# Another order of 1287 jobs in a sketched attention with attention experts behind it

## The chip, the core and the metric

The kernel runs on one core of a Trainium2 chip. Five engines work in parallel, each through its own list of instructions: PE (the tensor engine, with a separate row PEld for its weight loads), DVE (the vector engine), ACT (the scalar engine), POOL (GpSimd) and SP (which here only issues DMA transfers; ACT issues a few too). Engines wait for one another by semaphores. The metric is the device time of one execution in microseconds, lower being better.

## The reference

Two stages in float32. The first is an attention without softmax over sketched features, for 4 batches, 4 heads, 1088 positions and 32 dimensions; the second, on its output, is a layer of 4 attention experts of which every position uses two.

```python
def phi(x):                                   # r = 8, so 64 features
    a = np.einsum('rd,bhsd->bhsr', S1, x)
    b = np.einsum('rd,bhsd->bhsr', S2, x)
    return np.einsum('bhsi,bhsj->bhsij', a, b).reshape(*x.shape[:-1], r * r)
q_p, k_p = phi(q), phi(k)
kv = np.einsum('bhsf,bhsd->bhfd', k_p, v)
z = np.sum(k_p, axis=2)
x = num / (den + 1e-6)                        # num = q_p @ kv, den = q_p @ z
x = x.transpose(0, 2, 1, 3).reshape(4, 1088, 128)

logits = x @ w_gate                           # 4 experts, the best two
w = exp(sel - max(sel)); w /= w.sum(-1) + 1e-9
for e in range(4):
    q, k, v = x @ wq[e], x @ wk[e], x @ wv[e]
    a = causal softmax of q @ k.T / 8
    out += w[e, where chosen] * (a @ v @ wo[e])
```

The output is 4 x 1088 x 128.

## The kernel before

**A plan of jobs.** The kernel's body emits nothing at first. It describes 1287 jobs in a `Plan` (from line 64): each has a name, the engine or the two engines it may run on, the values it reads and makes, and the buffers it holds. Then `plan.run(ORDER)` (line 1316) walks a hand-placed string (lines 21 to 56) and emits the jobs in that order. A word of it is a job's number; a letter b behind it picks the second of the job's engines. An engine's program is thus the part of the list that falls to it, in the list's order, and the engine keeps to that order: an instruction that waits holds up all that stands behind it on the same engine. Buffers come from small pools (4 pairs of PSUM banks "ps", 6 row buffers "w", 3 "in", 3 "qs", 3 "mb", 2 "xT", 2 "AT", 2 "agg", 2 "ob" and so on). A job that first uses a buffer takes the one longest free, so the list also decides which buffer each job gets and whose release it waits for. The compiler adds separate event-semaphore instructions where an instruction has to wait for more than it can carry itself.

**The stages of a batch.** The jobs' names are used below.

- *Sketched attention.* "load k", "load q", "load v" (lines 429, 437, 457) bring rows in; "turn k" and "turn q" (490, 494) transpose them on DVE; "sketch" (524, PE) applies S1 and S2; "back" (527, DVE) transposes the sketches; in batches 1 to 3 "add low" (548, POOL) adds the two halves of the keys' sketch; "features" (532, POOL or DVE) forms the 64 products; "sums" (576, PE) gives kv and z; "numer" (635 or 771, PE) and a division give x. x is kept transposed ("xT") and is also stored to a scratch in memory and fetched back in another layout ("xra", "xrb", "xrc").
- *Gate.* "logits" (822 and 829, PE), "turn logits" (833, DVE), "choose" (856 to 872, DVE) finds the two experts, "maximum", "exponents" and "shares" (875 to 902) the weights, "turn choice" (922 to 926), and the choice goes through memory to become masks "mb" (947, 950). "gate order" (294, 295, POOL) brings the columns of `w_gate` ("wgr") into the order the gate uses.
- *Experts.* Rows go in tiles of 64, 17 a batch, in three groups: tiles 0 to 5, 6 to 11, 12 to 16; the last batch takes them in the order second, third, first. For each group "query" (1018, PE) multiplies x by a product of wq and wk for all four experts, "base" (a copy) and "pick" (1031, DVE) select by the masks. Then for each tile: "score" (1056, PE), "take" (1068, DVE: mask and running maximum), "exp" (1084, ACT), "guard" (1090 on ACT or 1092 on POOL: adds 1e-9), "invert" (1095, DVE), "weigh" (1099, POOL: times the inverse and the gate's share), "turn A" (1104, DVE: a 32 x 32 block transpose into "AT"). The group's "sum" jobs (1132, PE) multiply AT with x; they need all tiles of their group. "keep V", "patch V", "spread V", "mix V" (1162 to 1175) sort the results by expert, "out" (1210, 1236, 1260, PE) multiplies by a product of wv and wo, and the result is copied and stored.

Batches overlap: the sketched attention and the gate of a batch are woven into the experts of the batch before.

**The head of the list.** Among the first jobs are the loads, eight "dummy" jobs (251, two matmuls on zeros each), and setting-up work on POOL: constants, "pick8" (340 to 345), the mask (287, 290), "rep16" (348) and "skx" (349), clearings (479), and the gate order, which waits for the transfer of `w_gate` (271). In the compiled program a transfer waits for the one issued eight earlier.

**The names by number.** In a name such as "take 2.15.0" the first number is the batch, the second the tile and the third the part of the row; in "pick 0.1.1" and "sum 2.1.0" the second is the group.

Of the kernel before, what the change touches and what calls it, by code (L numbers as in the profile page):

```python
# [18 lines left out]


ORDER = """
1 3 0 2 48 76 77 4 74 51 37b 75 10a 60 46 52 84 50 81 54 49 88 8a 45 89 7a 17a 85 22a 78 80 97 86 79 53 87 400 98 100a
397 90 55 99 91 92 63b 83a 64 391 102a 47 101b 96a 392 66 103b 24a 19a 59 82a 65 67a 401 114 115a 396 39b 108 95a 94a
110 111a 93a 403 56 109a 112 113a 105 104 106a 394 116 58 402 406 107b 57 122 408 407 123 395 410a 117a 68 126 118 69
413a 409a 127 119 399a 61 128 120 398a 393 70 414b 124 129a 412a 405 416 121b 125a 411a 62a 415 404 146 147 152 688 148
154 417a 693 162 418 163 153 149 179 180 183a 155 150 424 425a 156 158 151 167 184a 131 168 181 157a 170 130 689 169
159a 185 419 182 426 186 201 700 164 9b 174 215 175 427 133 202 208 132 165 428 203 209 176 216 204a 171 429 205 430 246
222 245 166a 435 210 211a 223 436 217 187 206 694 172 431 207 433a 177 212 250a 691 194 432a 18a 249a 195 137 318 160
173 218a 188 319 247 699 697 437 189 219 213 196 248 161a 251 690 438a 197a 434 252 439a 323a 322a 190a 703 421 422 191
224 192 692 220 268 214 704 420 705 193 423 706a 267 71 698 134 72 269 276 707a 275 440 710a 73 277 135 270 324 320 225b  # L30
221 198 321 271b 708a 199 226 292 227 272 291 325 23b 278 695a 696a 293 200 178a 273 441 145 442a 31b 253 136 702 228
274 283 711a 443a 254 701 294 279a 28b 284 709a 260 326 280 327 295a 261 285 461 296 462 262 712 255 328 329 713 281
714a 229 230 330b 231 715 256a 297 263b 721 463 286 282 464 233b 466 235a 257 264 359 258 465 358 722a 471 716 298 140
234a 351 265 360 232a 141 237 236 259 238 266 350 989 334 335 467 287a 139 352 720 985 472 361 138 342 343 239 362 16b
331 723 468 288 336 344 353 289 363 332 991 290 476 479 337 724 345 477 725 333 364a 354b 355 480a 481b 726 478 356 365
299 14b 300 301 302 303 304 338a 482 483 143 241 346a 306a 366 339 340 732 990 444 142 367 448 307a 305a 718 341 473 347
447 445 733 505 446 474 308b 240 242 348 309 311 310 727 512 986 728 506 519 243b 994 312 513 545 520 514 349 498 499
515a 988 357 544 521 144 314 729a 491 516 996 313 38b 315 469 507 543 15b 542 734 992b 316a 546a 997 492 508b 475a 493
735a 494a 20b 517 368 26b 522a 736a 369 509 370 495 500 993a 371 372 451 719 547b 501b 29b 548 523 717 373 524 510 374
375 518 450 449 737 376 730b 484 731 549 525 377a 496 379a 502 503 244 378b 497 380a 485 383 589 588 486 550 382 381 738  # L40
452 511 11b 590 551 572 573 740a 564 574 384 487a 504 739a 565 488 575 576a 580 581 566 1000 489 582 758 615 490 591 577
1002 1004b 616 470 583 618 759 552 459 617 567 1001 526 568a 619a 578 1008a 592a 620a 584b 527 987 25b 762 1007b 1003a
569 453 621 768 579 1006a 528 529a 585 557 622 553a 530a 32b 531a 1005b 558 760 623 33b 593 624 317 625 586 533 761 385
1010 534 570 559 386 763 594 1009 626 1011a 627a 536 769 764 532b 554 535 587 648 1012 647 571 560a 639 628 640 649 595
765 774 999 629 631 561 630 562 458 641 632 460 773 778a 656 642 655 455 555 776 775 633 538 657 770 777a 643a 1013 563
634 995 650 658 644 779 651a 780 539 659 556 537 771 635b 540a 795 802 796 645 456 636 41b 387 652 653 660 454 1014 661a
803 637 646 662 816 1018 596 663 654 597 817 1019b 598 599 998 664 781 457 638 788 782 789 818 600 601 741 790 665 772a
804 819a 12b 602b 797 745 603b 744 791b 604a 820 541 792 605a 666 805b 607 821 742 608 806 667 606 1020 609 390 822 807
668 783 1017 1021 1022 40b 743 669 388 1023 670 766 1024 27b 1029 751 839 809 810 840 784b 1025 671 672 1030 43b 673 747
785 1026a 844a 808 748 841 843a 1027a 1031 1028 793 675a 786 842 1016 811 787 798b 676a 845 812a 612 677a 1015 1033a  # L50
1032a 749 846 389 13b 674a 794 756 813 678 679 611 799 800 854 885 1034 855 610 613a 750 35b 886 887 861 862 888 847 863
848 814 681 864 1035 1037b 815 878 801 680 856 877 870 869 849 34b 754 889b 857a 746 879 850a 913 912 871 1036a 1055 823
824 916b 872 1056 865b 1057 1058 890 851 1059 825 873a 6b 1065 917b 866 767 880 914 829a 1066 757 827a 915 918 752 858
828a 867 826a 881b 868 859 682 852 891 919 882 929 1060 830 853 928 937 874 892 875 831 936 883 1061 945 683 833 930 884
931 938 832 920 876 932b 921 753 953 614 922 860 21b 944 946 952 939 1063 947 1142 923 954 1141 1067 955 933 948a 1146a
1143 956 1144 893 949 1145a 686 1038 934 957 958a 894 940a 1039 1147 1148 959 960 895 935 896 897 898 901a 1172 1171 755
924b 950 900a 925 961 1041 42b 941 951 904 834 899a 835 926 1164 1163 902a 44b 927 1173 905 903 1040 1187 1042 1165 1149
1150 1188 1156 1189 36b 942 836 1190 906 1174 1191b 1215 943 1068 684 837b 1069a 687 1180 1151 1157 1158 1179 1192 1217
1181 1214 1159b 1216 962 1064 1182 963 1219b 1183b 964 1152b 965 1166 1044 1175a 1193 838 966 1160 1153 1167b 967 1184
1218a 1161 1220 1194 968 1185 969 1221 970 1168 1176 1222 1162 685 972a 973a 976 1255 971b 974a 1045 1154 1254 977 975  # L60
978 1177 1223 1155 1256 1257 1258 1230 1224 1178 1259 1047 1247 1225 1231 1246 1169 1071 1052 1046 1070 1248 1062 1186
907 1260a 1073 5b 1051 1232 1226b 1075a 1072 1043 1261 1262 909 1048 1074b 1238 1227 1249 908 1170 1076 1228 1050 1233
1077 1239 1106 1234a 910a 1240 1235 1229 1085 979 1236 1086 1107 911 1241 1250a 980 1242b 1251 1243 1108 1244 1245 1263
1113 1099 1195 1109a 1049 1252 1196 1100 1114 30b 1197 1087 1088a 1253 1198 1237 1078 1092 1054 1093 1115 1094 1079 1199
1200 1201b 1095b 1264 1096 1080 1265 1205 1266 1267 1204b 1116b 1110 1081b 1268 1053 1089 1117 1269 1082 983 1083 1202b
1090 1101 1203b 1111 1207 1091 1084 1270 1206 1208 981 1102a 1271 1103 1272 1118 1209 1112 1119 1210 1097 1273a 1274a
1104 1098 1105 982 1211 1278 1275b 1120 984 1121 1276a 1122 1123a 1277 1128 1279 1125 1280 1281 1126a 1212a 1127a 1213
1124 1131 1132 1133 1129 1282 1284 1283 1130a 1134 1139a 1285 1135b 1286 1140b 1136a 1137b 1138a
""".split()


# [1278 lines left out]
```

## Time and profile before

| what | value |
|---|---|
| runs | 259.37, 260.77 and 422.44 us, median 260.77 |
| the profiled execution's own time | 260.19 us |
| its span, first to last instruction | 258.5 us |
| granted clock of the tensor engine | 1.00 |
| PE idle, from the span | 9.1 us |
| the four largest lines on PE | L1056 73.7 us, L1132 44.6 and 27.2, L1018 34.3 |
| moved by transfers | 27.88 MB in 40381 packets |

The profile is of one execution. Its page gives busy time for each engine, the span in slices, the chain of work that ended last and the costliest groups of instructions; the trace behind it answers questions on stretches of time, on one line of the code or on one engine. "L1056" is a line of the kernel as it was before; in the changed kernel every line behind the list is one larger, since the list has one line more. Matmuls overlap one another, so a busy PE is not a PE at its peak.

### The profile page before, as it was taken

The numbers are of one execution on the slowest core, as the hardware profiler recorded it, in microseconds if no ns is written. First come the engines' busy times: TensorE is split into PE (matmuls) and PEld (weight loads), VectorE is DVE, ScalarE is ACT, GpSimd is POOL, SyncE is SP. The second block draws the span as 40 slices with busy tenths as digits, with TensorE's granted clock in tenths as the row PEclk, the third lists the DMA queues.
The fourth block names the chain that finished last, engine by engine and source line by source line (L and its number), as shares of the span: only waits on it lengthen the run. The fifth ranks groups of instructions, "written<-read, shape, count | busy, mean of one in ns | idle before, by whom it ended". The sixth has DMA issues, their size and how long they took to land.

```text
span 258.5 us, 9931 instructions
## 1 busy us (share of the span) xinstructions
PE 249.4 (96%) x4159; PEld 185.6 (72%) x4161; DVE 207.2 (80%) x527; ACT 108.0 (42%) x287; POOL 157.8 (61%) x265
## 2 busy tenths in 40 slices
PE   7888998999999999999999999999999999999995
PEld 2467654576598896665799776765896975789994
DVE  6969899998987886999997387999888638878332
ACT  4346445872803505840634044624624316432110
POOL 6718489958489754577663976087366634533742
PEclk9999999999999999999999999999999999999999
DMA  6936379205827552702612694304252157430003
GB/s 212 240 98 174 92 195 252 45 3 127 215 54 147 126 146 79 193 3 82 172 32 38 125 249 126 84 18 140 42 90 76 53 136 184 110 60 3 3 4 86
DMA packets 40381, 27.88 MB, mean 108 GB/s; under 512 B 25872, under 2 KB 35600, under 8 KB 40336
## 3 DMA queue, kind: packets, MB, share of 16 engines
q1 hardware_dynamic: 39888, 26.62, 42.8%
q8 instruction: 32, 0.52, 0.9%
q10 hardware_dynamic: 448, 0.62, 0.7%
q14 instruction: 13, 0.11, 0.1%
HBM read 22.62 MB, written 4.62 MB: 105 GB/s over the span
## 4 chain that ended last, share of the span: by engine, by line
PE 83%; DMA 6%; DVE 5%; POOL 2%; issue 2%; ACTq 0%; ACT 0%; DVEq 0%; POOLq 0%
PE pair L1132 30%; PE pair L1056 26%; PE pair L1018 9%; PE pair L1260 7%; PE pair L1210 3%; DMA wgr<-in_moe_w_gate_dram 2%; DMA w<-in_v_dram 2%; PE pair L771 2%; POOL fp L532 2%; DMA in<-in_q_dram 2%; PE pair L524 1%; PE pair L576 1%; DVE qs L1031 1%; PE pair L1236 1%; PE pair L822 1%
## 5 line engine op out<-in xcount | busy, mean ns | idle before, releaser
L1099 POOL TENSOR_SCALAR w<-w,rs,sh 128x960 f32<-128x960 f32 (+15 forms) x68 | 56.5, 837 | 32.1 <-DVE rs L1095 29.5
L1056 PE MATMUL pair<-xT,qs 128*128 128x320 f32 (+11 forms) x216 | 73.7, 478 | 1.3 <-DVE rs L1095 0.7
L1084 ACT ACTIVATE w<-w,mx 128x768 f32<-128x768 f32 (+16 forms) x68 | 52.3, 769 | 48.0 <-DVE mx L1068 44.3
L1068 DVE CUSTOM_DVE_ANT_0 w<-pair,mask 128x192 f32<-128x192 f32 (+14 forms) x68 | 48.3, 723 | 11.3 <-PE pair L1056 9.1
L1056 PEld LDWEIGHTS pair<-xT,qs 128*128 128x128 f32 x216 | 38.3, 190 | 26.5 <-issue 10.9
L1104 DVE STREAM_TRANSPOSE AT<-w 128x64 f32<-128x64 f32 (+15 forms) x68 | 50.7, 758 | 4.6 <-POOL w L1099 4.5
L1132 PE MATMUL pair<-AT,xra 32*128 32x160 f32 (+5 forms) x1136 | 44.6, 302 | 0.0
L1132 PEld LDWEIGHTS pair<-AT,xra 32*128 32x128 f32 x1136 | 41.8, 185 | 3.7 <-issue 1.5
L1166 POOL TENSOR_TENSOR agg<-agg,mb 128x768 f32<-128x768 f32 (+1 forms) x22 | 33.9, 1557 | 13.0 <-ACT agg L194 8.8
L1018 PE MATMUL pair<-xT,Mq 128*128 128x384 f32 (+1 forms) x96 | 34.3, 477 | 0.1
L194 ACT COPY agg<-pair 128x384 f32<-128x384 f32 (+1 forms) x34 | 14.1, 464 | 48.4 <-PE pair L1132 45.5
L532 POOL TENSOR_TENSOR fp<-w 128x576 f32<-128x576 f32 x22 | 26.6, 1223 | 2.8 <-DVE w L527 1.8
L1132 PE MATMUL pair<-AT,xrb 32*128 32x160 f32 (+5 forms) x752 | 27.2, 288 | 0.0
L1132 PEld LDWEIGHTS pair<-AT,xrb 32*128 32x128 f32 x752 | 26.3, 185 | 0.8 <-issue 0.7
L1031 DVE COPY_PREDICATED qs<-mb,pair 128x768 f32<-128x768 uint16 (+1 forms) x24 | 23.1, 964 | 2.6 <-DMA mb<-me 1.2
L1018 PEld LDWEIGHTS pair<-xT,Mq 128*128 128x128 f32 x96 | 17.3, 190 | 10.0 <-issue 2.1
L1260 PEld LDWEIGHTS pair<-Mo,agg 128*128 128x128 f32 x168 | 20.6, 192 | 3.2 <-issue 1.4
L1260 PE MATMUL pair<-Mo,agg 128*128 128x128 f32 x168 | 21.3, 277 | 0.0
L1092 POOL TENSOR_SCALAR rs<-zs 128x1 f32<-128x1 f32 x28 | 6.3, 226 | 20.8 <-ACT w L1084 17.9
L1162 DVE COPY_PREDICATED agg<-mb,pair 128x384 f32<-128x384 uint16 (+1 forms) x24 | 12.8, 554 | 6.5 <-ACT agg L194 6.3
L194 ACT COPY qs<-pair 128x384 f32<-128x384 f32 (+1 forms) x18 | 7.8, 459 | 16.4 <-PE pair L1018 16.4
L527 DVE STREAM_TRANSPOSE w<-pair 128x576 f32<-128x576 f32 x16 | 11.6, 755 | 3.2 <-PE pair L524 3.0
(173 smaller groups left out, 288.6 us busy)
## 6 DMA issues: line engine op xcount, KB each, us to landing
xra<-xd SPq DMA_DIRECT2D x16, 192.0 KB, 4.6
xrb<-xd SPq DMA_DIRECT2D x16, 192.0 KB, 4.8
xrc<-xd SPq DMA_DIRECT2D x16, 160.0 KB, 4.6
in<-in_k_dram SPq DMA_DIRECT2D x7, 272.0 KB, 4.4
mb<-me SPq DMA_DIRECT2D x3, 576.0 KB, 6.1
mb<-me SPq DMA_DIRECT2D x6, 288.0 KB, 3.9
in<-in_q_dram SPq DMA_DIRECT2D x3, 544.0 KB, 6.4
xd<-w SPq DMA_DIRECT2D x12, 136.0 KB, 3.1
```

The lines of the kernel that those rows point to most:

```text
L194: (nc.scalar.copy if eng == "ACT" else VEC[eng].tensor_copy)(o, i)
L532: VEC[e].tensor_tensor(out=f, in0=a[:, :, None, R : 2 * R].to_broadcast([128, NJ, R, R]), in1=a[:, :, 0:R, None].to_broadcast([128, NJ, R, ...
L1018: nc.tensor.matmul(plan[ps[x]][:, y, 0:w], Mq[:, ((1, 2), (0, 3))[x][y]], plan[xT][:, 64 * t0 : 64 * t1], start=True, stop=True)
L1031: nc.vector.copy_predicated(chosen(), c, rows(plan[ps[x]]))
L1056: nc.tensor.matmul(plan[p][:, y, 0 : c1 - c0], plan[qs][:, 128 * t : 128 * t + 128], plan[xT][:, c0:c1], start=True, stop=True)
L1068: nc.vector.tensor_tensor_reduce(out=o, in0=src, in1=msk, scale=-1.0, scalar=mx[:, b, i, x - 1 : x] if x else 3e38, op0=ALU.add, op1=ALU.m ...
L1084: nc.scalar.activation(out=a, in_=a, func=ACTF.Exp, bias=mx[:, b, i, last : last + 1], scale=-1.0, accum_out=zs[:, b, i : i + 1])
L1099: nc.gpsimd.tensor_scalar(out=a, in0=a, scalar1=rs[:, b, i : i + 1], scalar2=plan[("sh", b)][:, i : i + 1], op0=ALU.mult, op1=ALU.mult)
L1104: nc.vector.transpose(dst[:, 0 : keys // 32, t], plan[A][:, 0:keys].rearrange("p (j s) -> p j s", s=32))
L1132: nc.tensor.matmul(plan[Vk[g // 2]][:, g % 2, lo : 32 * nt], plan[(f"xr{j // 12}", b)][rows, j % 12], a[rows, j, lo:], start=(j == 0), sto ...
L1166: nc.gpsimd.tensor_tensor(out=a, in0=a, in1=masks_in(plan[mb], w)[:, 2 * x : 2 * x + 2], op=ALU.mult)
L1260: nc.tensor.matmul(plan[p][0:m, 0, 128 * x : 128 * x + 128], plan[agg][:, e, 128 * x : 128 * x + m], Mo[:, e], start=(e == 0), stop=(e == ...
```

## The change

Only the string `ORDER` is replaced. It holds the same 1287 jobs in another order, some with another letter: 15 guards move from ACT to POOL and 14 from POOL to ACT, seven "keep V" copies from ACT to DVE and nine back, five "base" copies from ACT to DVE and two back, and a few features, spreads, scalings and stores change sides. One dummy job more runs on PE (dummy18). No other line differs. The first and last lines of the two lists:

```diff
 ORDER = """
-1 3 0 2 48 76 77 4 74 51 37b 75 10a 60 46 52 84 50 81 54 49 88 8a 45 89 7a 17a 85 22a 78 80 97 86 79 53 87 400 98 100a
-397 90 55 99 91 92 63b 83a 64 391 102a 47 101b 96a 392 66 103b 24a 19a 59 82a 65 67a 401 114 115a 396 39b 108 95a 94a
...
-1104 1098 1105 982 1211 1278 1275b 1120 984 1121 1276a 1122 1123a 1277 1128 1279 1125 1280 1281 1126a 1212a 1127a 1213
-1124 1131 1132 1133 1129 1282 1284 1283 1130a 1134 1139a 1285 1135b 1286 1140b 1136a 1137b 1138a
+2 1 3 44b 76 77 0 45 74 401 46 75 48 52 8a 49 17a 78 79 7a 51 54 85 88 84 80 4 81 89 22a 50 86 34b 87 10a 97 98 90 64
+100a 53 99 91 391 19a 92 394 102a 63a 96a 395 402 59 101b 24a 56 82a 392 66 103b 83a 65 67a 95b 94a 93a 114 115a 403 110
...
+1207 981 1274a 1208 1119 1209 1275b 1278 1211 1084 1273a 1210 1120 1277 1121 1276b 1122 984 1212a 1123a 1280 1279 1128
+1125 1124 1281 1127a 1213 6b 1126a 1131 1129 1282 1284 1286 1130a 1132 1133 1134 1139a 1283 1135b 1137b 1285 1140b 1136a
+1138b
 """.split()
```

What the new list moves around the places of which the prediction speaks, by the lists of the engines:

- On SP, the load of `w_gate` (job 56) is the 14th transfer instead of the 16th, the two halves of batch 1's keys (jobs 391 and 392) the 11th and 15th instead of the 13th and 14th. Three more loads go by ACT in both.
- On POOL, the gate order stands ahead of pick8, the mask, rep16, skx and the clearing of batch 1's keys instead of behind them.
- On DVE, "take 2.15.0", "take 2.16.0", "choose b3.0" and "keep V 2.0.1" stand between "pick 2.2.0" and "turn A 2.7".
- At the end, ACT issues two of the last three stores, and SP one, instead of one and two.

More of the change, by code (lines that the diff above doesn't have):

```diff
@@ L27 @@
[L27 to L61, printed above, removed]
@@ L67 @@
-1104 1098 1105 982 1211 1278 1275b 1120 984 1121 1276a 1122 1123a 1277 1128 1279 1125 1280 1281 1126a 1212a 1127a 1213
-1124 1131 1132 1133 1129 1282 1284 1283 1130a 1134 1139a 1285 1135b 1286 1140b 1136a 1137b 1138a
+2 1 3 44b 76 77 0 45 74 401 46 75 48 52 8a 49 17a 78 79 7a 51 54 85 88 84 80 4 81 89 22a 50 86 34b 87 10a 97 98 90 64
+100a 53 99 91 391 19a 92 394 102a 63a 96a 395 402 59 101b 24a 56 82a 392 66 103b 83a 65 67a 95b 94a 93a 114 115a 403 110
+57 108 112 113a 111a 105 397 104 109a 58 396 400 107b 116 60 47 406 106b 55 122 408 407 68 393 123 117a 126 410a 413a
@@ new lines @@
+118 127 398a 119 61 70 399a 414b 69 128 409a 120 412a 405 62a 121b 129a 691 124 416 411a 125a 415 404 146 689 147 154
+152 148 179 162 180 153 155 417a 150 130 149 694 418 163 183a 424 131 156 425a 688 151 167 168 158 164 170 184a 181 169
+692 174 182 157a 159a 426 700 185 18a 175 30b 132 186 427 419 201 215 693 165 428 245 696a 187 202 216 171 423 133 176
+203 429 208 204a 435 166a 172 430 177 188 431 217 205 246 436 209 249a 250a 699 206 697 218a 222 207 33b 210 211a 194
+36b 195 422 248 432a 223 160 433a 247 219 319 437 212 213 161a 695a 196 135 420 438a 189 23a 439a 251 318 434 252 703
@@ new lines @@
+173 690 214 190b 323a 322a 267 704 197a 224 268 705 71 191 706a 198 708a 269 72 192 709a 324 440 270 193 199 271a 276
+275 277 272 178a 200 321 421 137 225b 273 226 73 227 136 278 291 320 707a 292 441 325 293 220 228 443a 284 134 279a 701
+442a 711a 283 698 274 260 280 285 221 991 294 261 710a 327 144 326 286 253 328 262 295b 287b 461 140 712 990 296 288 329
+254 713 281 702 289 255 31b 986 714b 994 229 297 263a 230 715 26b 231 716 462 721 463 256a 282 233a 264 464 235a 722a
+138 298 39b 359 232a 358 141 290 237 466 257 234a 360 989 351 14b 236 350 258 265 259 361 335 334 342 352 343 238 142
@@ new lines @@
+465 139 330b 12b 336 337 362 717 331 344 345 723 266 239 353 724 479 476 332 471 478 43b 725 472 477 299 363 333 726
+481a 364a 444 300 467 27b 985 480a 301 302 346a 468 727 482 338a 339 347 732 473 348 303 733 354a 304 365 483 447 734
+445 307a 13b 340 474 242 349 240 735b 355 306a 305b 356 310 341 308a 309 241 519 446 357 448 512 311 312 491 243a 366
+987 545 544 143 492 505 513 315 988 514 515a 475b 520 145 314 367 313 469 521 506 522a 523 498 316a 719 543 728 730b 317
+542 493 494a 507 499 368 720 547b 508a 369 370 495 736b 737 524 516 729a 40b 996 500 517 718 449 546b 496 371 372 373
@@ new lines @@
+455 374 997 375 376 454 525 501b 497 548 378a 549 518 509 731 484 377a 457 5b 485 993b 379a 510 502 381 451 380a 450 589
+588 382 486 503 504 590 550 487a 488 551 738 511 572 384 573 565 489 740b 574 564 739a 581 566 580 567 575 582 1000 9b
+583 591 383 490 568b 758 1002 615 759 762 1004a 552 576a 768 1001 616 1003b 618 458 592b 452 470 1006b 617 456 526 569
+760 620a 577 459 1007b 619a 578 593 621 527 769 622 992a 579 528 557 531a 532a 1005a 530a 1008a 534 584b 558 529b 594
+533 585 559 385 761 624 595 648 623 570 244 386 647 1010 625 626 553b 1009 560b 763 586 535 627a 649 764 628 587 650 571
@@ new lines @@
+640 639 536 773 561 651a 554 1011b 641 632 775 631 774 629 630 655 1012 656 765 20b 652 555 562 776 642 633 453 460 643a
+556 537 778a 563 657 539 634 644 777a 390 635a 1013 538 779 770 995 780 658 540a 795 1017 636 389 999 659 802 796 645
+803 660 637 653 646 804 816 1018 596 597 1016 1019a 771 661b 797 662 817 638 37b 788 654 789 772b 781 818 819b 598 663
+790 599 600 601 664 782 665 602a 666 604a 667 798b 1015 741 820 821 783 745 603b 799 16b 668 791a 606 605a 607 998 1020
+742 541 822 669 744 609 1021 608 792 1023 1022 743 793 839 766 809 1024 1029 840 805a 843b 747 670 810 1025 1014 784a
@@ new lines @@
+671 672 1027a 1026a 751 673 785 811 806 786 844b 841 1030 1031 842 845 1028 611 794 612 812a 677a 610 1033a 846 862
+1032a 674a 678 755 28b 676b 861 675a 1034 813 613b 807 814 863 800 787 847 679 387 815 864 848 885 886 1035 748 865b 680
+854 887 1036a 808 801 878 877 870 681 746 849 855 888 1037a 869 614 889b 879 912 871 752 880 913 1055 850a 917b 749 890
+1056 856 823 824 872 881a 866 867 1057 873b 1059 882 916b 874 825 767 851 914 918 42b 868 875 876 915 682 919 852 891
+937 936 853 883 1058 1065 756 827a 826a 830 829b 944 683 928 831 929 945 892 857a 750 753 828a 858 833 884 938 952 35b
@@ new lines @@
+930 953 1060 920 939 1061 859 832 946 1066 955 41b 921 954 931 932b 922 860 1144 32b 1141 1143 947 956 948a 940a 923
+1142 949 1067 941 933 893 957 1146a 950 1063 924b 25b 894 895 951 942 1068 388 1145a 925 1038 896 897 934 958b 11b 1147
+959 898 902a 960 1148 835 900a 686 926 1172 1040 901b 943 899a 836 905 903 904 935 1163 1164 1156 1165 906 1039 961 927
+1166 834 754 837a 1171 1173 1042 1187 1179 684 15b 1041 1157 1180 1181 1188 1189 38b 1182 1149 1174 1215 1214 1216 1150
+1167a 757 1217 1190 1064 1219a 962 1069b 963 1158 964 1218b 965 1151 1183a 966 1191a 1184 1168 967 968 1159b 969 1175a
@@ new lines @@
+1220 1169 1185 1176 970 1152b 1160 1221 1177 1186 1178 974a 973b 972a 971a 1223 1044 1254 1222 1161 977 975 1162 1257
+976 978 1047 1192 1224 1255 1225 1256 838 1070 1258 1071 1170 1193 1153 1231 1046 1154 1230 1247 1075b 1246 1074b 1259
+1194 908 1155 907 1248 1260a 909 1261 1226b 1227 685 1053 1073 687 1062 1052 1232 1072 1076 1043 1238 1233 1249 1077
+1239 910b 1050 1240 1228 1049 1262 1234b 1085 1045 1235 1229 1250a 1236 1086 1241 1242b 1106 1107 1251 979 29b 1252 980
+1263 1048 1108 1243 1099 1100 1109b 1087 1244 1253 1113 1195 1196 1197 1245 1198 1110 1078 1237 1114 1101 1115 1102b
@@ L69 @@
+1092 1093 1199 1200 1111 1103 1204a 1051 1079 1088b 1116a 1264 1089 1104 1265 1266 1105 1054 1202b 1201a 1205 1267 1112
+1268 983 1117 1269 1094 1095b 1080 1096 982 1270 1081a 1082 1271 1272 1118 1090 1097 911 1203a 1083 1091 1206 1098 21b
+1207 981 1274a 1208 1119 1209 1275b 1278 1211 1084 1273a 1210 1120 1277 1121 1276b 1122 984 1212a 1123a 1280 1279 1128
+1125 1124 1281 1127a 1213 6b 1126a 1131 1129 1282 1284 1286 1130a 1132 1133 1134 1139a 1283 1135b 1137b 1285 1140b 1136a
+1138b
 """.split()
```

8 lines of the change are left out of this document (removed).

## The prediction

> **What bounds the kernel now.** I read the page's first part and its chain by engine, then the windows of five microseconds, then the chain in order of time.
>
> ```profile
> span 258.5 us, 9931 instructions
> PE 249.4 (96%) x4159; PEld 185.6 (72%) x4161; DVE 207.2 (80%) x527; ACT 108.0 (42%) x287; POOL 157.8 (61%) x265
> PE 83%; DMA 6%; DVE 5%; POOL 2%; issue 2%; ACTq 0%; ACT 0%; DVEq 0%; POOLq 0%
> ```
>
> The tensor engine (PE) is busy for 249.4 of 258.5 us and is 83% of the chain that ended last. An average hides stages, so the windows come next; the columns are PE, weight load, DVE, ACT, POOL, granted clock, DMA share and GB/s.
>
> ```profile
> 30.00:35.00 5.00, 4.44 (x74) 2.30 (x74) 4.80 (x15) 1.50 (x4) 3.25 (x13) 1.00 0.23 55
> 35.00:40.00 5.00, 4.95 (x22) 3.11 (x23) 4.92 (x22) 4.12 (x16) 4.57 (x10) 1.00 1.03 282
> 40.00:45.00 5.00, 4.23 (x50) 2.18 (x49) 4.89 (x9) 2.12 (x9) 5.00 (x9) 1.00 1.13 235
> 45.00:50.00 5.00, 5.00 (x77) 2.81 (x75) 5.00 (x12) 3.73 (x9) 4.67 (x8) 1.00 0.36 64
> 205.00:210.00 5.00, 5.00 (x161) 4.96 (x153) 0.84 (x4) 0.00 (x0) 0.84 (x2) 1.00 0.66 169
> 210.00:215.00 5.00, 5.00 (x17) 2.82 (x16) 3.84 (x9) 1.48 (x4) 3.74 (x4) 1.00 0.24 72
> 250.00:255.00 5.00, 5.00 (x39) 4.33 (x37) 2.66 (x5) 1.34 (x3) 1.83 (x2) 1.00 0.23 56
> ```
>
> All 42 windows from 45 to 255 us, of which four stand here, have PE at 5.00. Ahead of 45 us PE has holes and DVE is full (4.80, 4.92, 4.89). So there are three stages: a head, a long stage in which PE never stops, and a tail. The chain in order of time gives the joints.
>
> ```profile
> 10.79 5.82 DMA wgr<-in_moe_w_gate_dram
> ...
> 19.59 0.80 POOL w L548
> ...
> 25.35 0.83 PE pair L576 x67
> ...
> 26.62 0.39 DVE ch L833
> ...
> 42.45 1.24 PE pair L1056 x4
> ```
>
> The gate's weights land at 10.79 + 5.82 = 16.61. POOL then prepares the keys of batch 1 from 19.59 on (add low, features), the sums at 25.35 need them, the first gate logits follow, and DVE turns these at 26.62. From there DVE works without a pause until the query selection "pick 0.1.1", which the scores at 42.45 wait for. From 42.45 on PE runs through. A reordering can therefore win in the 42 us of the head and in the last 3 us. In between it can only lose, unless PE's own instructions get shorter or fewer.
>
> **The change part by part.** The listings of the two compiled kernels show the same 1287 jobs. PE has one dummy more and otherwise the same jobs: 258 from "sketch k2" on in both, 136 of them at the same place, the others moved by one place in the mean and eight at most, with 48 changes of tile mode in both. About 60 jobs change their engine: 15 guards go from ACT to POOL and 14 back, and DVE gets 391 jobs instead of 384. The event-semaphore instructions are 43 instead of 48 on PE, 101 instead of 98 on DVE, 77 instead of 65 on ACT.
>
> *The head's transfers and POOL.* Among all loads (three go by ACT) the gate's weights are the seventeenth instead of the nineteenth; the halves of batch 1's keys, which were sixteenth and seventeenth, are fourteenth and eighteenth. POOL takes up the weights first, and only then does five jobs that stood ahead of them.
>
> ```profile
> 8.91 0.88 SPq L429 DMA_DIRECT2D in<-in_k_dram  x2
> 10.24 0.33 SPq L437 DMA_DIRECT2D vr<-in_v_dram  x1
> ```
> ```profile
> 16.16 1.37 DVE L490 STREAM_TRANSPOSE in<-in 128x544 f32<-128x544 f32 x2 [1.08 <-DMA in<-in_k_dram]
> ```
> ```profile
> 0.79 0.11 POOL L340 MEMSET pick<- 128x16 f32 x1 [0.29 <-POOLq L1334]
> ...
> 1.67 0.20 POOL L345 MEMSET S2r<- 128x128 f32 x1
> ...
> 5.46 0.95 POOL L287 MEMSET mask<- 128x1024 bf16 x1
> 6.48 0.52 POOL L290 TENSOR_SCALAR_AFFINE_SELECT mask<-mask 64x64 bf16<-64x64 bf16 x2
> ...
> 12.19 0.15 POOL L479 MEMSET in<- 128x64 f32 x1
> 12.28 0.84 POOL L348 COPY rep<-SK 32x256 f32<-32x256 f32 x1
> 13.07 0.73 POOL L349 COPY skx<-SK 128x32 f32<-128x32 f32 x1
> 16.66 0.18 POOL L294 COPY wg<-wgr 128x2 f32<-128x2 f32 x1 [2.87 <-DMA wgr<-in_moe_w_gate_dram]
> 16.78 0.18 POOL L295 COPY wg<-wgr 128x2 f32<-128x2 f32 x1
> ```
>
> The seventeenth issue is the second of the pair at 8.91, so about 8.91 + 0.44 = 9.35. With the same 5.82 of flight the weights land at 15.17. Behind that wait POOL now has: the gate order (16.66 to 16.96, 0.30), the repeated sketch and skx (12.28 to 13.80, 1.52), a clearing (0.09, from 12.19 to the next start), the pick matrix and S2r (0.79 to 1.87, 1.08) and the mask (5.46 to 7.00, 1.54). That is 4.53 us, so add low starts at 15.17 + 4.53 = 19.70 instead of 19.59: +0.1. If the transfer lands where it did, the start is 16.61 + 4.53 = 21.14, +1.6. The keys are the other limit. Their second half went out at 9.35, and DVE turned both halves at 16.16 when they were there, so 6.81 later; now it goes out in the eighteenth slot, 10.24: 17.05, 0.9 later. The turning of the first half no longer stands behind that wait, so only half of 1.37 follows it: ready at 17.05 + 0.69 = 17.74 instead of 17.53, and add low with it at 19.59 + 0.2 = 19.8. If the keys' flight is shorter now that their halves are apart, nothing but the sketch and the weights limits, and I bound that gain at 0.5, a slot between two issues (10.79 − 10.24). I take the later of the two limits, +0.2, because the lists move the starts and the rows give the flights. The five POOL jobs from add low on keep their order.
>
> *DVE from the first gate logits to pick 0.1.1.* It does the same 34 jobs in another order, with nine semaphore instructions ahead of them instead of eight.
>
> ```profile
> L1056 PEldq EVENT_SEMAPHORE  x5: 51/51/51, 96.2 to 223.1; - x5
> ```
> ```profile
> L1068 DVEq EVENT_SEMAPHORE  x44: 21/21/1605, 38.0 to 234.1; - x44
> ```
>
> These are the least, median and longest nanoseconds; the 1605 is a wait, the 21 the instruction. One more is +0.02. In the three windows from 30 to 45 DVE idles 0.20 + 0.08 + 0.11 = 0.39, so no order of the same jobs can win over 0.4 there; a new wait in it could cost, which is a rival. I take 0.0.
>
> *PE from 42.45 on.* The same work, back to back. From "sketch k2" on two semaphore instructions fewer, at the 51 ns of such a row: −0.1. If PE's queue takes them during running matmuls it is nothing; if all five saved counted it would be −0.26. The Trainium skill ("Perfetto Trace Analysis", Identifying Dependency Chains) says that instructions that wait on several engines may get event-semaphore instructions inserted ahead of them. By that rule the twelve more on ACT and three more on DVE are real waits of several engines and not only 21 ns each; the trace's row agrees in so far as 21 is the usual price and 1605 has been seen.
>
> *The extra dummy* lies ahead of the scores at 42.45, where PE idles 0.56 + 0.05 + 0.77 = 1.38 us between 30 and 45.
>
> ```profile
> L251 PE MATMUL pair<-idle 128*128 128x512 bf16 x14 | 5.1, 499 | 1.5 <-DVE idle L244 1.2 <-DVE w L527 0.3
> L1092 POOL TENSOR_SCALAR rs<-zs 128x1 f32<-128x1 f32 x28 | 6.3, 226 | 20.8 <-ACT w L1084 17.9 <-ACT rs L1090 1.5
> ```
>
> Its two matmuls cost 2 x 0.50 = 1.0 us and fit in: nothing. If the holes are gone, +1.0. *The engine swaps*: one guard more on POOL at 0.23 us, seven jobs more on DVE at its mean of 207.2 / 384 = 0.54, 3.8 us on an engine that idles 258.5 − 207.2 = 51 us. PE's stream covers them; where that cover is thin is the second rival.
>
> *The tail.* Before, SP issues the first two of the last three stores and ACT the third; now ACT issues two.
>
> ```profile
> 255.50 0.83 SPq L1242 DMA_DIRECT2D out_dram<-ob  x2
> 255.74 0.35 ACTq L1242 DMA_DIRECT2D out_dram<-ob  x1
> ```
>
> The last issue ends at 255.74 + 2 x 0.35 = 256.44 instead of 255.50 + 0.83 = 256.33: +0.1; with the issues free in another order, −0.1 to +0.35.
>
> **Sum.** 258.5 + 0.2 + 0.0 − 0.1 + 0.0 + 0.1 = 258.7 us of span. The profiled execution took 260.19 with a span of 258.5, so 1.69 lie around it: 260.4. The median of the runs before, 260.77, is 0.2% above the profiled one; I forecast beside the profiled one.
>
> **The rivals.**
> *Weights late* (+1.6 in the head in place of +0.2): the flight of 5.82 is long for a small transfer, so it may hang on what else is in flight and not on the issue. 261.8 us.
>
> *Small gains*: the head's −0.5, the tail's −0.1, the five semaphores' −0.26 and DVE's 0.4 make −1.3 at most; 0.9 of it gives 259.3.
>
> *Slower, a sum that waits for its turned attention.* In batch 2 the sums "2.1.0" start on PE at 182.81 and need the block that DVE turns at 178.60.
>
> ```profile
> 178.60 0.71 DVE L1104 STREAM_TRANSPOSE AT<-w 128x512 f32<-128x512 f32 x1
> 179.23 1.19 DVE L1068 CUSTOM_DVE_ANT_0 w<-pair,mask 128x1024 f32<-128x1024 f32 x1
> 180.35 0.95 DVE L1068 CUSTOM_DVE_ANT_0 w<-pair,mask 128x768 f32<-128x768 f32 x1
> ```
> ```profile
> 166.89 0.19 DVE L868 TENSOR_TENSOR c<-ch 128x9 bf16<-128x9 f32 x1
> ...
> 167.37 0.22 DVE L872 TENSOR_TENSOR c<-c 128x18 bf16<-128x18 bf16 x1
> ```
> ```profile
> L1095 DVE RECIPROCAL rs<-rs 128x1 f32<-128x1 f32 x68 | 8.5, 141 | 3.0 <-POOL rs L1092 1.6 <-ACT rs L1090 1.4
> ```
> ```profile
> 182.81 3.37 PE L1132 MATMUL pair<-AT,xra 32*128 32x192 f32 x76
> ```
>
> Cover now: 182.81 − 179.31 = 3.5 us. The new list puts four more DVE jobs between the query selection "pick 2.2.0" and this block: the two maskings in these rows, of the group after (179.23 to 181.30, 2.07 us), the second half of a choice (166.89 to 167.59, 0.70) and a copy at the mean of 0.54; two reciprocals of 0.14 fall out. PE has the same jobs ahead of the sums as before. Left: 3.5 − 3.31 + 0.28 = 0.5 us, a little more where the choice, no longer ahead of the selection, lets that begin earlier. So the sums stall as soon as DVE is more than 0.5 late there, each microsecond beyond it is one on the end, and there are some nine such entries in batches 1 to 3. If the covers of all nine are eaten so and each loses 0.7 more, the size of one small DVE job, PE loses 6.3: 266.6. For it: DVE has more jobs, and its covers are thin. Against it: PE is at 5.00 in all windows though such entries exist now, and DVE idles enough to catch up between them (3.84 and 0.84 of 5.00 in the two windows from 205 on). If only one or two entries slip, it is 0.7 to 2.5 us: 262.0 for the middle.
>
> *Faster.* In the window from 210 PE shows 5.00 while its weight load shows 2.82, so a busy PE there is not at its limit: with the next weights ready sooner, more interleaving could shorten it. If the 2.2 us of every 5 us shrank by a tenth of it in half of the 210 us, it would be 0.22 x 21 = 4.6, and with the small gains −5.5: 254.8. Against it: 48 changes of mode and one place of mean movement leave the neighbours of nearly every matmul alike, and in the window from 205 the load is at 4.96. The Trainium skill ("Perfetto Trace Analysis", Identifying the Most-Contended Engine) says that matmul busy time is a poor measure of headroom and that the busy share of weight loads should be used; by it PE stands at 72%, not 96%, and 72.9 us would be open to a better order. The two windows show that this holds in some stretches and not in others.
>
> That the change does nothing is excluded: the listings differ on every engine.
>
> **How the numbers follow.** Forecast 0.56 (own range 260.1 to 261.7: the sum with the tail's and the dummy's bounds), small gains 0.12, weights late 0.10, one or two slips 0.11, many slips 0.08, faster 0.03. About 2%, 5.2 us, is what a measurement of this kernel can tell from no change; it puts the bounds at 255.6 and 266.0. So faster 0.03, slower 0.08, within 0.89. The range from 258.3 to 263.0 goes 1 us past the small gains and 1 us past weights late and the slips, which can fall together; it leaves out faster and many slips, 0.11, and the ends of the others.
>
> **What would show it.** Right: PE at 5.00 in all windows from 45 to 255, scores starting at 42.2 to 42.8, add low near 19.8, the weights' flight still near 5.8. Weights late: POOL's wait for them ends at 16.6 and the first scores at 44. Slips: rows of PE or its weight load waiting on DVE's AT (L1104) ahead of L1132. Wrong altogether: the same matmuls with other mean times.

## The result, and the profile after

| | before | after |
|---|---|---|
| median of 16 runs each | 260.72 us (258.37 to 422.44) | 261.49 us (260.96 to 263.2) |
| the profiled execution, and its span | 260.19, 258.5 | 260.96, 259.2 |
| ratio, after to before | | 1.0055, 95% interval 1.0029 to 1.0081 |

The change makes the kernel 0.3 to 0.8% slower, about 1.4 us at the middle of the interval. That is less than 2%, but clear of zero, and the forecast (260.4 beside a profiled 260.19, 0.2 us more) named a seventh of it. The ratio is that of the means, 261.64 to 260.22 us, without the two disturbed runs of before (264.44 and 422.44).

The page of the profile after, first part, and its chain by engine:

```profile
span 259.2 us, 9943 instructions
PE 249.8 (96%) x4161; PEld 185.7 (72%) x4163; DVE 212.9 (82%) x543; ACT 106.6 (41%) x281; POOL 154.7 (60%) x255
...
PE 82%; DMA 7%; DVE 5%; POOL 2%; issue 1%; ACT 1%; SPq 0%; ACTq 0%; DVEq 0%; POOLq 0%
```

Windows of five microseconds after (columns as in the prediction):

```profile
35.00:40.00 5.00, 4.62 (x21) 2.87 (x20) 4.79 (x24) 3.55 (x12) 4.67 (x11) 1.00 0.95 211
40.00:45.00 5.00, 4.75 (x53) 2.56 (x52) 4.87 (x9) 3.56 (x12) 4.42 (x8) 1.00 1.17 237
45.00:50.00 5.00, 4.81 (x76) 2.66 (x74) 4.86 (x12) 2.29 (x7) 4.74 (x8) 1.00 0.96 181
180.00:185.00 5.00, 5.00 (x62) 3.50 (x63) 3.61 (x11) 4.10 (x10) 3.77 (x11) 1.00 0.51 139
```

From 50 to 255 us PE is at 5.00 in every window, as before. The one window past 45 with a hole is 45 to 50 (4.81, before 5.00). The window from 180 holds the place of the slower rival, and no stall is in it. So whatever is lost is lost ahead of 50 us or behind 255.

Comparing the traces at places that both lists pass with the same work behind them: numer 1 (the first multiplication of batch 1's features with its sums) ends at 49.57 before and 50.09 after; the last matmul ends at 255.37 and 255.48; the span ends at 258.47 and 259.24. One execution each thus shows +0.5 in the head, −0.4 in the middle, +0.7 in the tail. The runs say +1.4 in the mean, so one execution each isn't enough to tell where the loss is. That is what the experiments are for.

### The profile page after: what moved, and what is told of

Read it like the earlier page. It is cut to its first block, busy times and chain, and to the rows that moved or that the text cites. A ratio compares the mean times of both kernels' runs of the same rounds, so it can differ in the third digit from the quotient of the medians.

```text
span 259.2 us, 9943 instructions
## 1 busy us (share of the span) xinstructions
PE 249.8 (96%) x4161; PEld 185.7 (72%) x4163; DVE 212.9 (82%) x543; ACT 106.6 (41%) x281; POOL 154.7 (60%) x255
## 4 chain that ended last, share of the span: by engine, by line
PE 82%; DMA 7%; DVE 5%; POOL 2%; issue 1%; ACT 1%; SPq 0%; ACTq 0%; DVEq 0%; POOLq 0%
PE pair L1133 30%; PE pair L1057 24%; PE pair L1019 9%; PE pair L1261 7%; PE pair L1211 3%; DMA w<-in_v_dram 2%; PE pair L577 2%; DMA kvr<-kd 2%; PE pair L525 2%; PE pair L772 2%; POOL fp L533 2%; DMA in<-in_q_dram 1%; DVE qs L1032 1%; PE pair L1237 1%; DVE w L528 1%
## 5 line engine op out<-in xcount | busy, mean ns | idle before, releaser
L1100 POOL TENSOR_SCALAR w<-w,rs,sh 128x320 f32<-128x320 f32 (+14 forms) x68 | 56.6, 838 | 40.8 <-DVE rs L1096 35.4
L1085 ACT ACTIVATE w<-w,mx 128x256 f32<-128x256 f32 (+14 forms) x68 | 52.4, 772 | 57.6 <-DVE mx L1069 43.7
L1057 PE MATMUL pair<-xT,qs 128*128 128x384 f32 (+11 forms) x216 | 73.2, 476 | 0.9 <-DVE qs L1032 0.9
L1105 DVE STREAM_TRANSPOSE AT<-w 128x448 f32<-128x448 f32 (+15 forms) x68 | 50.6, 757 | 3.5 <-POOL w L1100 3.4
L1069 DVE CUSTOM_DVE_ANT_0 w<-pair,mask 128x192 f32<-128x192 f32 (+15 forms) x68 | 48.2, 722 | 5.2 <-PE pair L1057 3.9
L195 ACT COPY agg<-pair 128x384 f32<-128x384 f32 (+1 forms) x36 | 15.2, 466 | 57.3 <-PE pair L1133 48.4
L533 POOL TENSOR_TENSOR fp<-w 128x576 f32<-128x576 f32 x21 | 26.0, 1254 | 3.0 <-DVE w L528 2.6
L1261 PEld LDWEIGHTS pair<-Mo,agg 128*128 128x128 f32 x168 | 19.9, 192 | 1.8 <-issue 1.0
L1261 PE MATMUL pair<-Mo,agg 128*128 128x128 f32 x168 | 20.5, 277 | 0.0
L195 DVE COPY agg<-pair 128x384 f32<-128x384 f32 (+1 forms) x10 | 5.3, 528 | 11.0 <-PE pair L1133 8.8
```

The lines of the kernel that those rows point to most:

```text
L195: (nc.scalar.copy if eng == "ACT" else VEC[eng].tensor_copy)(o, i)
L533: VEC[e].tensor_tensor(out=f, in0=a[:, :, None, R : 2 * R].to_broadcast([128, NJ, R, R]), in1=a[:, :, 0:R, None].to_broadcast([128, NJ, R, ...
L1057: nc.tensor.matmul(plan[p][:, y, 0 : c1 - c0], plan[qs][:, 128 * t : 128 * t + 128], plan[xT][:, c0:c1], start=True, stop=True)
L1069: nc.vector.tensor_tensor_reduce(out=o, in0=src, in1=msk, scale=-1.0, scalar=mx[:, b, i, x - 1 : x] if x else 3e38, op0=ALU.add, op1=ALU.m ...
L1085: nc.scalar.activation(out=a, in_=a, func=ACTF.Exp, bias=mx[:, b, i, last : last + 1], scale=-1.0, accum_out=zs[:, b, i : i + 1])
L1100: nc.gpsimd.tensor_scalar(out=a, in0=a, scalar1=rs[:, b, i : i + 1], scalar2=plan[("sh", b)][:, i : i + 1], op0=ALU.mult, op1=ALU.mult)
```

## The experiments

A first theory put the loss where the two profiles show it: in the tail. Its rival put it in the head. Four kernels splice the two lists, and every ratio below is to the kernel before, measured together with it; NEW and OLD are the lists of after and before, and the sets of jobs are closed, so each splice is a valid order.

```diff
 # new_tail
-NEW
+OLD[:1270] + NEW[1270:]
 # old_tail
+NEW[:1270] + OLD[1270:]
 # new_head     (S = the jobs of OLD[:292], up to numer 1)
+[w for w in NEW if w in S] + [w for w in OLD if w not in S]
 # old_head
+[w for w in OLD if w in S] + [w for w in NEW if w not in S]
```

> The list of before with only its last 17 jobs in the new order (two of the last three stores issued by ACT, one by SP). Theory: the second store behind another on ACT costs about half a microsecond in the tail, so the last matmul ends at 255.4 as before and the span is 259.0 instead of 258.5; timed, 0.5 us slower than before (ratio 1.002). Rival (the tail costs the 0.1 of the forecast, the loss is in the head): span 258.6, ratio 1.000.

Measured: ratio 0.9995 (0.9966 to 1.0025), span 257.4. Nothing is lost that this can resolve.

> The new list with only its last 17 jobs in the old order. Theory: the new kernel's time less half a microsecond, span 258.6, timed ratio to before 1.002 to 1.003. Rival: nothing gained, ratio 1.005, span 259.1.

Measured: ratio 1.0044 (1.0017 to 1.0071), span 259.1. By the middle of the interval the old tail takes little of the loss away.

> The 292 jobs up to numer 1 (the first 50 us) in the new order, all others in the old one. Theory: numer 1 ends 0.2 to 0.5 us later (49.8 to 50.1), a part of it is regained where PE waited before, span 258.6 to 258.9, ratio 1.001 to 1.002. Rival (the head is the cause, and other executions lose more in it than the profiled one): ratio 1.004 or more.

Measured: ratio 1.0085 (1.0055 to 1.0115), span 259.2. The head alone is slower than the whole change.

> The same 292 jobs in the old order, all others, with the tail, in the new one. Theory: numer 1 ends at 49.6 as before, the middle gains 0.1 to 0.4 us, the tail loses half a microsecond: span 258.6 to 258.9, ratio 1.000 to 1.002. Rival (head is the cause): ratio 1.000 to 1.001; second rival (the middle is the cause in other executions): 1.004 or more.

Measured: ratio 1.0005 (0.9974 to 1.0036), span 258.4. With the old head no loss is left that this can resolve.

The interval of new_head decides: it leaves out the 1.001 to 1.002 of the first theory. The other three lean the same way, though their intervals also hold what that theory expected. The four were measured together, and their medians fall by the head and not by the tail: 259.43 and 259.67 us with the old head (new_tail, old_head), 260.82 and 261.79 with the new one (old_tail, new_head). So the head is the main cause.

The profiles also show that in the one profile of before the keys came late, though its time, 260.19, is not above the median. With the same old head, sketch k1 (PE's sketch of batch 1's keys) started at 17.68 in it, and at 16.98 in new_tail:

```profile
17.68 0.78 PE L524 MATMUL pair<-in,SKk 32*32 32x288 f32 x32 [0.93 <-DVE in L490]
```
```profile
16.98 0.78 PE L525 MATMUL pair<-in,SKk 32*32 32x288 f32 x32 [0.56 <-DVE in L491]
```

In both, PE waits for DVE's turned keys (L490, or L491 with the longer list), and DVE for the keys' transfer. So it is in four of the five profiles with the old front (17.43 in old_head, 17.48 in old_front): it is as fast as the keys land. In the fifth, old_head_tail, PE started without a wait, at 17.18. In the kernels with the new front it is another thing. PE of after, and PE of before:

```profile
12.53 0.44 PE L385 MATMUL pair<-ident,AT 128*128 128x128 f32 x2 [0.93 <-DMA AT<-in_moe_wk_dram]
...
17.57 0.77 PE L525 MATMUL pair<-in,SKk 32*32 32x288 f32 x32
```
```profile
11.88 0.44 PE L384 MATMUL pair<-ident,AT 128*128 128x128 f32 x2 [0.48 <-DMA AT<-in_moe_wk_dram]
```

After, sketch k1 starts at 17.57 with no idle time ahead of it: PE is late with its own list. The same start is 17.41 in old_tail and 17.58 in new_head, again with no idle time ahead. Its list is late because the weights' transfer is, and because ACT is. ACT of after, and ACT of before:

```profile
11.94 1.57 ACT L195 COPY vp<-w 128x1024 f32<-128x1024 f32 x3 [7.78 <-DMA w<-in_v_dram]
13.54 0.80 ACT L195 COPY AT<-pair 128x768 f32<-128x768 f32 x1
```
```profile
10.24 0.30 ACT L194 COPY vp<-w 32x128 f32<-32x128 f32 x1 [3.39 <-DMA w<-in_v_dram]
10.80 0.29 ACT L194 COPY vp<-w 32x128 f32<-32x128 f32 x1 [0.26 <-DMA w<-in_v_dram]
11.45 1.06 ACT L194 COPY vp<-w 128x1024 f32<-128x1024 f32 x1 [0.35 <-DMA w<-in_v_dram]
12.41 0.79 ACT L194 COPY AT<-pair 128x768 f32<-128x768 f32 x1
```

Before, the two small copies of v ran while the last quarters were still in flight; after, the large one stands first, so ACT waits for all quarters, and everything behind it, the copy of the turned weights and the turned features that PE's sums need, starts 1.1 us later (13.54 against 12.41). Two kernels test that, one in each direction.

```diff
 # v_back: in NEW; v_new is the reverse edit in OLD (names of jobs)
-SP, fifth to ninth:  load v0.0  load v0.1  load w2  load v0.2  load v0.3
+SP, fifth to ninth:  load v0.3  load w2  load v0.0  load v0.2  load v0.1
-ACT:  spread v0  spread v1
+ACT:  spread v1  spread v0
```

> The new list with the first ten transfers of SP in the old order (the last quarter of v of batch 0 fifth, not ninth) and, on ACT, spread v1 ahead of spread v0 again. Theory (in the head PE comes late to sketch k1, since turn qf waits for ACT, which waits for v): ACT's copy of the turned weights starts at about 12.5 instead of 13.5, PE is ready for sketch k1 at 17.0 instead of 17.57, then the keys' second half limits it at 17.0 to 17.4; 0.2 to 0.5 us gained, ratio 1.002 to 1.005. Rival (the first part of the head is no worse than before, only the second is): nothing gained, ratio 1.005 to 1.008.

Measured: ratio 1.0031 (1.0006 to 1.0056). ACT and PE of v_back:

```profile
12.20 0.79 ACT L195 COPY AT<-pair 128x768 f32<-128x768 f32 x1
```
```profile
17.08 0.77 PE L525 MATMUL pair<-in,SKk 32*32 32x288 f32 x32
```

Sketch k1 starts 0.5 earlier, as expected. In time the difference to 1.0055 is inside both intervals: the gain is not shown there. Its numer 1 still ends at 49.95, because in this execution PE paused for 0.4 in the gate's logits, for which the trace names no releaser; the profiles of old_front and old_head_tail have a like pause at the same place.

> The list of before with only the first ten transfers of SP and the two spreads of v on ACT in the new order. Theory: ACT's copy of the turned weights starts at 13.5 instead of 12.4, PE is ready for sketch k1 at 17.3 to 17.6 instead of 16.8, so sketch k1 starts there even when the keys are early: 0.3 to 0.6 us slower, ratio 1.001 to 1.002. Rival (the keys limit anyway): 1.000.

Measured: ratio 1.0045 (1.0014 to 1.0077). DVE and PE of v_new:

```profile
15.56 1.37 DVE L491 STREAM_TRANSPOSE in<-in 128x544 f32<-128x544 f32 x2 [0.68 <-DMA in<-in_k_dram]
```
```profile
17.40 0.77 PE L525 MATMUL pair<-in,SKk 32*32 32x288 f32 x32
```

The keys are turned by 15.56 + 1.37 = 16.93, and sketch k1 starts at 17.40: with the old list around it, the small edit makes PE the limit. The traces show the mechanism in both directions; in time only the loss of v_new is clear of zero. It is more than expected; the interval includes the expected size. Each edit moves the weights' transfer and ACT's copies together, so how much is due to which stays open.

Two further edits in the new list looked at other suspects.

```diff
 # gate_behind (POOL)
-gate order  rep16  clear k1  pick8  mask  add low 1.1
+rep16  clear k1  pick8  mask  gate order  add low 1.1
 # dve_back (DVE)
-turn k2.1  pick 0.0.0  pick 0.0.1
+pick 0.0.0  pick 0.0.1  turn k2.1
-pick 0.2.0  ...  take 0.9.0
+...  take 0.9.0  pick 0.2.0
 # all_back: v_back, gate_behind and dve_back together
```

> The new list with the gate order, which waits for the gate's weights, behind the mask on POOL instead of ahead of five jobs. Theory (sketch k1 needs a clearing that stands behind this wait, and in executions in which the weights land later than in the profiled ones all of the head slips): the slow executions up to 263.2 go, the median falls by 0.3 to 0.7, ratio 1.001 to 1.004; in the profile sketch k1 may start as before at 17.4 to 17.6. Rival (POOL has room): same times as the new list, ratio 1.005 to 1.006.

Measured: ratio 1.0041 (1.0014 to 1.0067), longest run 262.44, sketch k1 at 17.57. The difference to 1.0055 is inside both intervals, so a gain is not shown.

> The new list with two DVE jobs where the old one has them: turn k2.1 behind both first selections (pick 0.0.0 and 0.0.1), pick 0.2.0 behind take 0.9.0. Theory (numer 1 waits for the PSUM pair that take 0.9.0 reads): numer 1 starts without a wait, and ends 23.0 to 23.2 us after the first turned gate logits start instead of the 23.5 of the three profiles with the new head (22.95 with the old); 0.3 to 0.5 gained, ratio 1.002 to 1.004. Rival (DVE is full there, so an order of the same jobs moves nothing): 23.5, ratio 1.005.

Measured (six runs): ratio 1.0099 (1.0062 to 1.0137); numer 1 ends 24.7 us after the first turned logits. A miss, and a useful one. PE of dve_back:

```profile
45.93 0.70 PE L1019 MATMUL pair<-xT,Mq 128*128 128x320 f32 x2
47.92 0.91 PE L1057 MATMUL pair<-xT,qs 128*128 128x384 f32 x2 [1.29 <-DVE mx L1069]
```

The selection pick 0.2.0 frees a pair of PSUM banks, and the next score takes the pair longest free. With the selection behind the mask of tile 9, the score waits 1.29 us for that mask instead. The edit moved a wait from numer 1 to a job ahead of it and made it longer. The other half of the edit, turn k2.1, moved nothing: the scores of tile 8 start 16.07 after the first turned logits, and 16.05 in the kernel after. The early selection in the new list is right for the rest of the new list.

> All three edits together in the new list; the rest of the new list, its tail and its extra dummy stay. If these are the causes: numer 1 ends at 49.0 to 49.4, ratio 0.998 to 1.001, as for the kernel with the whole old head (1.0005). If the head has another cause: ratio 1.003 or more.

Measured: ratio 1.0072 (1.0048 to 1.0097), sketch k1 at 17.03, numer 1 at 50.73. The gain of v_back is there and the loss of dve_back covers it, so this kernel doesn't tell whether the causes are complete. Splitting the head does:

```diff
 # old_front    (T = the jobs of OLD[:124], up to the first turned gate logits, about 26 us)
+[w for w in OLD if w in T] + [w for w in NEW if w not in T]
 # old_second
+[w for w in NEW if w in T] + [w for w in OLD if w in S and not in T] + [w for w in NEW if w not in S]
 # old_head_tail
+old_head[:1270] + OLD[1270:]
```

> The new list with only the 124 jobs up to the first turned gate logits (the first 26 us) in the old order. Theory (the head loses in two places, 0.5 to 0.6 in this front against the usual execution of the old list, and 0.5 between the gate logits and numer 1): turned logits start at 25.9 to 26.4, numer 1 ends 23.5 later, ratio 1.002 to 1.003. Rival (all of it is in the front): 1.000.

Measured: ratio 1.0027 (1.0002 to 1.0051). The turned logits start at 26.40, as expected; numer 1 ends 24.1 later and not 23.5, with the pause in the logits that v_back shows.

> The new list with only the 168 jobs behind those, up to numer 1, in the old order (the second part of the head, 26 to 50 us). Theory: turned logits at 26.4 to 26.6 as in the new list, numer 1 ends 23.0 later instead of 23.5, ratio 1.002 to 1.004. Rival (all in the front): 1.005.

Measured: ratio 1.0027 (1.0002 to 1.0052), numer 1 ends 22.95 after the first turned logits.

By the middles of the intervals, either half of the head, put back, takes about half of 1.0055 away. The rival that puts all of it in the front falls by a hair: it expected 1.000 of old_front, whose interval ends at 1.0002, and 1.005 of old_second, which is still inside. The traces speak more plainly. The second half shows itself in every profile as the time from the first turned logits to the end of numer 1: 22.92 to 22.98 in the five profiles with the old second part and no pause in the logits (before, new_tail, v_new, old_head, old_second), 23.48 to 23.51 in the four with the new one (after, old_tail, new_head, gate_behind). In the first half the difference is smaller beside the spread: the turned logits start at 25.93 to 26.62 in the five profiles with the old front, 26.30 in the mean, and at 26.44 to 26.78 in the six with the new front and the new order of v (after, old_tail, new_head, gate_behind, dve_back, old_second), 26.60 in the mean.

> Old head and old tail around the new middle (50 to 250 us). If the new middle is worth the 0.2 us by which its profiles are shorter from numer 1 to the last matmul, and the old tail 0.3: ratio 0.998 to 1.000. Rival (the middle of both lists takes the same): 1.000.

Measured: ratio 0.9974 (0.995 to 0.9998), median 259.42 against 259.85 measured together. The new middle between the old head and the old tail has the lowest ratio of the kernels here, and is faster than before by a hair. Its runs lie close together (259.21 to 260.07), and all of them are shorter than every run of old_front (from 260.23) and of old_second (from 260.16), which were measured with it and have one half of the head, and the tail, new. The profiles don't show what the middle gains: from the end of numer 1 to the last matmul the four with the old middle take 205.1 to 206.0 us, the ten with the new one 205.3 to 205.6.

## Why the prediction was wrong

**That PE's long stage bounds the kernel and leaves only head and tail: right.** PE is at 5.00 from 50 to 255 in both, and the head decides. The time, 261.49, also lies inside the forecast's own range of 260.1 to 261.7, but that is luck: the range was made of the tail's and the dummy's bounds, and most of the loss came from two terms of the head.

**The head's transfers and POOL, +0.2: the first step that failed.** It set two limits for add low, the gate's weights and the keys, and took the later. It left out the third thing that sketch k1 waits for, PE's own list ahead of it, with ACT's copies of v behind five rearranged transfers. That limit moved from 16.75 (where PE began to wait in the profile of before, 17.68 − 0.93; 17.18 at the latest, in old_head_tail) to 17.4 to 17.75. Beside the profiled execution this hardly shows, since there the keys were late anyway (17.68); beside the execution with the earliest keys (16.98) it costs 0.4 to 0.8, and by the means of the turned logits above 0.3. So the base was wrong as well: a limit that varies from execution to execution was read off one execution, and the latest of five.

The two limits that were set came out too late: POOL was through with the mask at 19.04 and not at 19.70, and the keys were turned at 17.29 and not at 17.74. Add low started at 19.56, level with before, and not at 19.8. POOL of after:

```profile
15.65 0.19 POOL L295 COPY wg<-wgr 128x2 f32<-128x2 f32 x1 [2.45 <-DMA wgr<-in_moe_w_gate_dram]
...
15.90 0.39 POOL L349 COPY rep<-SK 32x256 f32<-32x256 f32 x1
16.24 0.20 POOL L350 COPY skx<-SK 128x32 f32<-128x32 f32 x1
...
17.49 0.95 POOL L288 MEMSET mask<- 128x1024 bf16 x1
18.52 0.52 POOL L291 TENSOR_SCALAR_AFFINE_SELECT mask<-mask 64x64 bf16<-64x64 bf16 x2
19.56 0.80 POOL L549 TENSOR_TENSOR w<-w 128x288 f32<-128x288 f32 x1 [0.52 <-DVE w L528]
```

From the gate order to the end of the mask it is 18.52 + 0.52 − 15.65 = 3.4 us, where the sum had 4.53, and add low waits for DVE (0.52), not for POOL.

**DVE from the logits to pick 0.1.1, 0.0: the second step that failed, too small by 0.2.** The same DVE jobs in another order ended 0.2 later: the scores of tile 8 start 16.05 after the first turned logits, 42.66 − 26.61, instead of 15.83, 42.45 − 26.62. Which job of the new order costs this, no run shows; by dve_back it is not turn k2.1. PE of after, and PE of before:

```profile
42.66 1.24 PE L1057 MATMUL pair<-xT,qs 128*128 128x288 f32 x4 [0.25 <-DVE qs L1032]
```
```profile
42.45 1.24 PE L1056 MATMUL pair<-xT,qs 128*128 128x288 f32 x4 [0.74 <-DVE rs L1095]
```

**PE from 42.45 on, −0.1: the same step, too small by another 0.3.** The head was taken to end at these scores. It goes on to numer 1, and there another 0.3 is lost, 0.5 in all since the turned logits. In the one pair of profiles the 0.4 that the middle is shorter by hides it, and the term comes out at −0.1 by luck; the other profiles listed above show the 0.5 again and the 0.4 not. What two semaphore instructions fewer are worth, no run shows. DVE and PE of after, then DVE and PE of before:

```profile
45.19 0.88 DVE L1032 COPY_PREDICATED qs<-mb,pair 128x640 f32<-128x640 uint16 x1
...
47.59 0.82 DVE L1069 CUSTOM_DVE_ANT_0 w<-pair,mask 128x640 f32<-128x640 f32 x1
```
```profile
48.48 1.63 PE L772 MATMUL pair<-fp,kvr 32*32 32x288 f32 x64 [0.19 <-DVE mx L1069]
```
```profile
46.32 0.79 DVE L1068 CUSTOM_DVE_ANT_0 w<-pair,mask 128x640 f32<-128x640 f32 x1
```
```profile
48.02 1.57 PE L771 MATMUL pair<-fp,kvr 32*32 32x288 f32 x64
```

In the new list the selection (45.19) stands ahead of the mask of tile 9, which ends at 48.4 instead of 47.1, and numer 1 waits for the PSUM pair that this mask reads. The wait of 0.19 is in the row; that it is the cause of the remaining 0.3 is argued, since the one edit that removed it made another wait.

**The extra dummy, nothing: right.** Its 0.4 us lies in front of the scores of tile 8, and PE idles 0.25 there instead of 0.74.

**The tail, +0.1: too small by 0.3 in the profiles.** SP and ACT at the end of after:

```profile
255.62 0.36 SPq L1243 DMA_DIRECT2D out_dram<-ob  x1
255.86 0.86 ACTq L1243 DMA_DIRECT2D out_dram<-ob  x2
```

The second store on ACT took 0.50 to issue and not the 0.35 of a single one, so the last issue ended 1.24 behind the last matmul instead of 0.96. From the last matmul to the end, five profiles with the old tail have 3.10 to 3.56, nine with the new one 3.33 to 3.78; in the means 3.26 and 3.69. The timed pair (new_tail, 0.9995) is too coarse to show 0.4.

**The rivals.** Weights late: POOL's wait for them ended at 15.65, a microsecond earlier than before, so no slip. Slower by a starved sum: the cover left at sum 2.1.0 was enough; PE is 0.11 us behind the profile of before, unchanged, from 164 us to 255. Faster: the order of PE's neighbours gave nothing that shows in PE's means (score matmuls 476 ns after, 478 before), though by the row of weight loads it is 72% loaded in both. By the Trainium skill ("Perfetto Trace Analysis", Identifying the Most-Contended Engine) this 72%, with the share of peak arithmetic, would be the measure of headroom; no run here found any of it by reordering, and the orders run here leave the neighbours of most matmuls alike.

Two of the rivals' times are off by a tenth: 260.4 + 6.3 is 266.7, and 260.4 − 5.5 is 254.9.

**The sum.** By the means of the profiles the front of the head costs 0.30 (26.60 − 26.30), its second part 0.55 (23.50 − 22.95) and the tail 0.43 (3.69 − 3.26), and the middle gives 0.1 back (205.5 and 205.4): 1.2 us, where the interval of the runs is 0.8 to 2.1 and the forecast was 0.2. By the times it is 0.28% for either half of the head, 0.25% at most for the tail (new_tail) and −0.26% for the middle (old_head_tail), each give or take about 0.25%. What the tail and the middle are worth in the times stays open.

## What to carry to other kernels

Read a limit that hangs on transfers from several executions (the same old front passed sketch k1 at 16.98 to 17.68), and ask what the next limit is at their best, not at the profiled one: a list with a late chain of its own loses every execution in which transfers were early. For each consumer in a start-up, list all its queues, its own engine's included: the engine that waits now may be the limit once its list is longer by a wait far upstream. Where buffers rotate, moving one job back to its old place in a new list is no undoing; put back whole closed stretches to find a cause.

## What the runs showed of the hardware

The two POOL copies that stood at 0.84 and 0.73 us before (12.28 and 13.07, while DVE formed features from 11.35 to 15.08) took 0.39 and 0.20 after, when DVE mostly waited, and by their starts 0.34 and 0.15 instead of 0.79 and at least 0.73. A clearing of 128 x 64 that stood beside the features (12.19) took 0.15, as it did at 5.37 ahead of them. The Trainium skill ("SBUF — State Buffer", SBUF: two separate sides) says that DVE instructions with two inputs from this memory and GpSimd instructions that read it hold a shared port in turn and block each other. The rows agree: copies that read became faster by half and more, a clearing that reads nothing did not. The list of gate_behind, which brings POOL's jobs back beside the features, shows it once more: there the first copy took 0.92 (13.12, beside features), but the second 0.20 (13.99, beside the turning of keys, which has one input), and the two AFFINE_SELECT instructions of pick8 took 1.42 (14.40, beside features again) instead of the 0.48 of the kernel after. So a POOL duration holds only for what DVE does beside it. The sum of 4.53 us was a third too long, and 1.0 of the 1.1 us too much are these two copies, whose times were taken from beside a busy DVE.
